# q weights in two requests ahead of x tiles 2 and 3, s one block behind y, and all reciprocals spread by way of DRAM

## Chip, cores and metric

The kernel runs on one core of one Trainium2 chip. The metric is the time of one execution on the device in microseconds (us). All times compared here are of undisturbed ("fast") runs.

## The reference

A layernorm of x feeds two branches, whose product is added to x. Branch A is attention with 32 heads of 16, over a window of 8 positions that are 2 apart. Branch B is a gated feed-forward net.

```python
x = A_x                                        # 1 x 2048 x 512, bf16
xn = _layernorm(x, axis=-1)
# branch A: idx = pos - 2 * [0..7], masked below 0
qkv = xn @ wqkv                                # 512 -> 3 * 512
logits = einsum("bhsd,bhswd->bhsw", q, k[idx]) * 16 ** -0.5
o = einsum("bhsw,bhswd->bhsd", softmax(logits), v[idx])
s = o @ wo                                     # 512 -> 512
# branch B
h = gelu(xn @ w_gate) * (xn @ w_up)            # 512 -> 1792
g = silu(h @ w_down)                           # 1792 -> 512
return x + s * g
```

## The kernel before

The 2048 positions are cut in two ways. A *tile of x* is 128 positions (there are 16: statistics, normalisation and transposition go by these). A *stage tile* is 512 positions, four tiles of x; there are four stage tiles, and for each of them the kernel does q/k/v, the attention sums, gate and up products ("glu"), and then, block by block of 128 positions, the down product y and the output product s. The order on each engine is the program's own: nothing is rescheduled. An engine takes its instructions in that order.

The loads, all issued in one queue by SyncE:

```python
for t in range(TPQ - 1):                 # x tiles 0, 1, 2: 128 KB each
    load_x(t)
load_w(wqkv_sb, A_wqkv, 0, D)            # q weights, 512 KB
load_x(TPQ - 1)                          # x tile 3
for i in range(1, 3):                    # k weights, v weights
    load_w(wqkv_sb, A_wqkv, i * D, (i + 1) * D)
load_x(TPQ, TPQ)                         # x tiles 4 to 7, then gate and up weights ...
```

The start-up. `warm_up` is idle matmuls, put there so that TensorE's clock comes up early (in the profile before, its matmuls of 128 columns start 0.106 us apart at 4.63 us and 0.056 us apart at 5.37). `first_moments` puts the statistics on VectorE and a square root on ScalarE. `transpose` is four transposes on TensorE into one PSUM tile, and a copy out of it, by ScalarE unless another is named; with `parts=2` the copy is made in two halves.

```python
first_moments(0); first_moments(1)
first_normalize(0)
transpose(0)
first_normalize(1)
warm_up(4, P)
transpose(1, parts=2)
warm_up(4, P)
first_moments(2); first_moments(3)
first_normalize(2); first_normalize(3)
# q of x tiles 0 and 1: 16 matmuls of 256 columns
...
transpose(HT, copy=nc.vector.tensor_copy)            # x tile 2
for fo in range(NC, 2 * NC):                         # k of x tiles 0 and 1
    qkv(0, fo, 0, HQ)
    if fo == NC:
        transpose(HT + 1, copy=nc.vector.tensor_copy)    # x tile 3
...
for fo in range(2 * NC):                             # q and k of x tiles 2 and 3
    qkv(0, fo, HQ, HQ)
```

The attention division: `denominators` sums the exponentials on TensorE and takes reciprocals on VectorE; these stand on 32 rows by head and have to be spread to all rows. For stage tiles 0 to 2 this goes through DRAM, for the last one by four matmuls:

```python
def spread_reciprocals(j):               # last stage tile
    sp = mm.tile([P, TQ], F32, name="sp_ps", tag="mm")
    for q in range(4):
        nc.tensor.matmul(sp[:, q * P : (q + 1) * P], lhsT=spread[:, q, :], rhs=st[j]["rs"][:], ...)
    rb = op.tile([P, TQ], F32, name="rb")
    nc.scalar.activation(out=rb[:], in_=sp[:], func=AF.Copy)

def spread_by_dma(j):                    # the others
    nc.sync.dma_start(out=rs_d[j][:, :], in_=st[j]["rs"][:])
    for i in range(WL):
        nc.sync.dma_start(out=rb[...], in_=rs_d[j]...)
```

The last stage, for each block of 128 positions:

```python
def down(j, tt):
    # y: 14 matmuls of 512 columns; sl = silu(y) on ScalarE
    # s: 4 matmuls of 512 columns from oT (the divided attention) and wo
    # m = s * sl, o_t = m + x on VectorE; store
```

The softmax here doesn't subtract the row's maximum and nothing guards it: scores larger than these inputs give would overflow.

## Time and profile before

| | before |
|---|---|
| time, median of 3 runs | 230.13 us (230.06 to 230.57) |
| span of the profiled execution | 228.7 us |
| TensorE busy, matmuls | 223.6 us, 98% |
| first q matmul | 7.00 us |
| first transpose of x tile 2 | 8.82 us |
| first k matmul | 9.06 us |
| first gate matmul | 18.20 us |

The last four rows are read from the timeline of TensorE. From the first gate matmul on TensorE has nearly no hole, so a delay at that station is a delay at the end. Two of the rows in the words of the timeline (start, length, engine, source line, operation, what it writes and reads, shape, count):

```profile
9.06 0.60 PE L247 MATMUL qkv_ps<-xnT,wqkv_sb 128*128 128x256 bf16 x4
...
18.20 1.03 PE L247 MATMUL g_ps<-xnT,wg_sb 128*128 128x512 bf16 x4
```

The DMA queue in the same start-up, from the view of busy time by stretch. The columns are the stretch and its length, then busy us and number of instructions of TensorE, its weight loads, VectorE, ScalarE and GpSimd, the granted clock, the busy share of the DMA engines, and GB/s moved.

```profile
3.50:4.50 1.00, 1.00 (x7) 0.67 (x5) 0.93 (x5) 0.29 (x1) 0.00 (x0) 1.00 0.78 115
4.50:7.00 2.50, 1.75 (x23) 1.27 (x21) 1.80 (x7) 1.66 (x5) 0.00 (x0) 1.00 1.03 359
```

The rate dips around 4 us, and is near 360 in the second stretch.

### The profile page before, as it was taken

The numbers are of one execution on the slowest core, as the hardware profiler recorded it, in microseconds if no ns is written. First come the engines' busy times: TensorE is split into PE (matmuls) and PEld (weight loads), VectorE is DVE, ScalarE is ACT, GpSimd is POOL, SyncE is SP. The second block draws the span as 40 slices with busy tenths as digits, with TensorE's granted clock in tenths as the row PEclk, the third lists the DMA queues.
The fourth block names the chain that finished last, engine by engine and source line by source line (L and its number), as shares of the span: only waits on it lengthen the run. The fifth ranks groups of instructions, "written<-read, shape, count | busy, mean of one in ns | idle before, by whom it ended". The sixth has DMA issues, their size and how long they took to land.

```text
span 228.7 us, 3538 instructions
## 1 busy us (share of the span) xinstructions
PE 223.6 (98%) x1324; PEld 106.3 (46%) x1324; DVE 147.6 (65%) x234; ACT 130.2 (57%) x214; POOL 23.0 (10%) x61
## 2 busy tenths in 40 slices
PE   8899999999999999999999999999999999999993
PEld 6764444444444444444444444444444444444453
DVE  4584996896995198865677169735549429945232
ACT  4679769764413866467621786747642396748211
POOL 1048973000000000110000000000000000000000
PEclk9999999999999999999999999999999999999999
DMA  6999589982378211110275711110147800000001
GB/s 163 359 373 371 140 170 199 242 204 75 109 172 197 55 24 29 26 29 0 92 175 135 170 25 28 26 34 0 45 120 165 203 26 3 0 0 4 23 23 46
DMA packets 30545, 24.46 MB, mean 107 GB/s; under 512 B 10176, under 2 KB 30528, under 8 KB 30528
## 3 DMA queue, kind: packets, MB, share of 16 engines
q1 hardware_dynamic: 30528, 24.24, 41.9%
q8 instruction: 10, 0.16, 0.3%
q14 instruction: 7, 0.06, 0.1%
HBM read 18.61 MB, written 4.31 MB: 100 GB/s over the span
## 4 chain that ended last, share of the span: by engine, by line
PE 94%; DMA 2%; ACT 1%; SPq 1%; DVE 0%; issue 0%; DVEq 0%
PE y_ps L416 21%; PE u_ps L247 21%; PE g_ps L247 21%; PE qkv_ps L247 17%; PE s_ps L426 6%; PE L_ps L304 3%; PE o_ps L375 3%; DMA wqkv_sb<-in_A_wqkv_dram 2%; PE q_ps L247 1%; ACT L400 1%; SPq L85 1%; PE den_ps L324 0%; ACT ge L400 0%; ACT vst L271 0%; PE tr L212 0%; ACT xnT L221 0%
## 5 line engine op out<-in xcount | busy, mean ns | idle before, releaser
L247 PE MATMUL g_ps<-xnT,wg_sb 128*128 128x512 bf16 x224 | 57.6, 379 | 0.0
L247 PE MATMUL u_ps<-xnT,wu_sb 128*128 128x512 bf16 x224 | 57.5, 379 | 0.0
L416 PE MATMUL y_ps<-wd_sb,h 128*128 128x512 bf16 (+1 forms) x238 | 51.2, 366 | 0.0
L404 DVE TENSOR_TENSOR h<-ge,u 128x512 bf16<-128x512 bf16 x56 | 23.8, 425 | 37.1 <-ACT u L402 36.4
L293 DVE TENSOR_TENSOR pk<-q_sb,k_sb 128x2048 bf16<-128x2048 bf16 x32 | 37.8, 1221 | 7.0 <-ACT k_sb L268 7.0
L402 ACT ACTIVATE u<-u_ps 128x512 bf16<-128x512 f32 x56 | 33.5, 599 | 14.7 <-PE u_ps L247 14.7
L400 ACT ACTIVATE ge<-g_ps 128x512 bf16<-128x512 f32 x56 | 33.5, 599 | 14.7 <-PE g_ps L247 14.4
L247 PE MATMUL qkv_ps<-xnT,wqkv_sb 128*128 128x512 bf16 (+1 forms) x208 | 40.9, 355 | 0.0
L361 DVE TENSOR_TENSOR pv<-E,v_arr 128x2048 bf16<-128x2048 bf16 x32 | 38.6, 1216 | 0.0
L416 PEld LDWEIGHTS <-h 128*128 128x128 bf16 x238 | 23.3, 98 | 25.3
L423 ACT ACTIVATE sl<-y_ps 128x512 bf16<-128x512 f32 (+1 forms) x17 | 9.7, 572 | 44.0 <-PE y_ps L416 44.0
L247 PEld LDWEIGHTS <-wu_sb 128*128 128x128 bf16 x224 | 21.9, 98 | 26.7 <-issue 0.3
L247 PEld LDWEIGHTS <-wg_sb 128*128 128x128 bf16 x224 | 21.2, 98 | 27.1 <-issue 3.0
L247 PEld LDWEIGHTS <-wqkv_sb 128*128 128x128 bf16 x224 | 21.6, 98 | 20.2 <-DMA wqkv_sb<-in_A_wqkv_dram 0.9
L434 DVE TENSOR_TENSOR m<-s_ps,sl 128x512 bf16<-128x512 f32 (+1 forms) x17 | 11.2, 658 | 24.2 <-PE s_ps L426 24.1
L426 PE MATMUL s_ps<-wo_sb,oT 128*128 128x512 bf16 (+1 forms) x68 | 16.6, 366 | 0.0
L197 POOL TENSOR_TENSOR rstd<-rstd,mhalf 128x1 f32<-128x1 f32 x12 | 7.7, 638 | 77.4 <-DVE rstd L194 75.2
L271 ACT ACTIVATE vst<-qkv_ps 128x512 bf16<-128x512 f32 x16 | 9.6, 597 | 6.4 <-PE qkv_ps L247 6.4
L268 ACT ACTIVATE k_sb<-qkv_ps 128x512 bf16<-128x512 f32 (+1 forms) x20 | 10.2, 514 | 3.5 <-PE qkv_ps L247 3.2
L265 ACT ACTIVATE q_sb<-qkv_ps 128x512 bf16<-128x512 f32 (+1 forms) x16 | 8.7, 544 | 3.6 <-PE qkv_ps L247 3.3
L426 PEld LDWEIGHTS <-oT 128*128 128x128 bf16 x68 | 6.6, 98 | 7.2
L159 POOL COPY spread<-ident 32x32 bf16<-32x32 bf16 x16 | 9.7, 646 | 0.2
(52 smaller groups left out, 115.8 us busy)
## 6 DMA issues: line engine op xcount, KB each, us to landing
v_arr<-vT SPq DMA_DIRECT2D x16, 520.0 KB, 5.1
vT<-vst SPq DMA_DIRECT2D x16, 128.0 KB, 2.1
out_dram<-o_t SPq DMA_DIRECT2D x15, 128.0 KB, 2.3
wg_sb<-in_B_w_gate_dram SPq DMA_DIRECT2D x2, 896.0 KB, 10.9
wu_sb<-in_B_w_up_dram SPq DMA_DIRECT2D x2, 896.0 KB, 12.7
wd_sb<-in_B_w_down_dram SPq DMA_DIRECT2D x1, 1792.0 KB, 13.7
wqkv_sb<-in_A_wqkv_dram SPq DMA_DIRECT2D x3, 512.0 KB, 5.6
x_sb<-in_A_x_dram SPq DMA_DIRECT2D x3, 512.0 KB, 11.4
```

Source lines behind the costliest of these rows:

```text
L159: nc.gpsimd.tensor_copy(out=spread[H * q : H * (q + 1), q, H * j : H * (j + 1)], in_=ident[H * q : H * (q + 1), H * q : H * (q + 1)],)
L247: nc.tensor.matmul(ps, lhsT=w[:, dk, lo : lo + P], rhs=xnT[j][:, dk, i0 : i0 + n], start=(dk == 0), stop=(dk == NC - 1),)
L268: nc.scalar.activation(out=k_sb[:, c, lo : lo + n], in_=ps, func=AF.Copy)
L293: nc.vector.tensor_tensor(out=pk[:], in0=st[j]["q"][:], in1=k_sb[:, :, off : off + TQ], op=ALU.mult)
L361: nc.vector.tensor_tensor(out=pv[:], in0=st[j]["E"][:, wh, :].unsqueeze(1).to_broadcast([P, 4, TQ]), in1=st[j]["va"][:, 4 * g : 4 * g + 4, ...
L400: nc.scalar.activation(out=ge[:], in_=g_ps[:], func=AF.Gelu_apprx_tanh)
L402: nc.scalar.activation(out=u[:], in_=u_ps[:], func=AF.Copy)
L404: nc.vector.tensor_tensor(out=h[:], in0=ge[:], in1=u[:], op=ALU.mult)
L416: nc.tensor.matmul(y[:], lhsT=st[j][fc][:, tt * P : (tt + 1) * P], rhs=wd_sb[:, fc, cols], start=(fc == 0), stop=(fc == NF - 1),)
L423: nc.scalar.activation(out=sl[:, cols], in_=y[:], func=AF.Silu)
L426: nc.tensor.matmul(s[:], lhsT=st[j]["oT"][:, g, tt * P : (tt + 1) * P], rhs=wo_sb[:, g, cols], start=(g == 0), stop=(g == NC - 1),)
L434: nc.vector.tensor_tensor(out=m[:], in0=s[:], in1=sl[:, cols], op=ALU.mult)
```

## The change

Its intent: the first matmul earlier (half of the q weights is asked for before x tile 2, and the last transposed tile is copied by two engines); fewer mode changes on TensorE (denominators and attention sums of stage tile 0 next to each other); four matmuls less (the last reciprocals go through DRAM as well); and s of a block one block later, so that it need not wait for its division. The core of the diff:

```diff
-    for t in range(TPQ - 1):
-        load_x(t)
-    load_w(wqkv_sb, A_wqkv, 0, D)
-    load_x(TPQ - 1)
+    load_x(0)
+    load_x(1)
+    load_w(wqkv_sb, A_wqkv, 0, D, 0, 2)      # rows 0 to 255 of the q weights
+    load_w(wqkv_sb, A_wqkv, 0, D, 2, 4)      # rows 256 to 511
+    load_x(2, 2)                             # x tiles 2 and 3 in one request
 ...
-            if copy is None:
+            if copy is None or k % 2:
                 nc.scalar.activation(out=dst[:, c], in_=src[:, c], func=AF.Copy)
             else:
                 copy(out=dst[:, c], in_=src[:, c])
 ...  # (the matmuls and the constants of spread_reciprocals go; every stage tile uses DRAM)
-    at(("qkv", 1, 3), denominators, 0)
-    at(("qkv", 1, 3), spread_by_dma, 0)
-    at(("qkv", 1, 10), av_sums, 0)
-    at(("qkv", 1, 10), divide, 0)
+    at(("qkv", 1, 8), denominators, 0)
+    at(("qkv", 1, 8), av_sums, 0)
+    at(("qkv", 1, 8), store_reciprocals, 0)
+    at(("qkv", 1, 10), spread_reciprocals, 0)
+    at(("down", 0, 0), divide, 0)
 ...
-    transpose(1, parts=2)
+    transpose(1, parts=2, copy=nc.vector.tensor_copy)
 ...
-    transpose(HT, copy=nc.vector.tensor_copy)
     for fo in range(NC, 2 * NC):
         qkv(0, fo, 0, HQ)
-        if fo == NC:
-            transpose(HT + 1, copy=nc.vector.tensor_copy)
+        if fo < NC + 2:
+            transpose(HT + fo - NC, copy=nc.vector.tensor_copy)
 ...  # down() is split: y and its silu in down(), s, product, sum and store in finish()
+        todo = []
         for tt in range(TPQ):
             run("down", j, tt)
-            down(j, tt)
+            ...
+                sl = down(j, tt, cols)
+                if todo:
+                    finish(*todo.pop())
+                ...
+                    todo.append((j, tt, cols, sl))
```

Cut from it: the new place of three pk products and some pv products on VectorE, and the last block, whose two halves keep the old order.

More of the change, by code (lines that the diff above doesn't have):

```diff
@@ L81 @@
     vT = dram.tile([D, SV], BF16, name="vT")
-    rs_d = [dram.tile([P, P], BF16, name=f"rs_d{j}") for j in range(NJ - 1)]
+    rs_d = [dram.tile([P, P], BF16, name=f"rs_d{j}") for j in range(NJ)]
     def load_x(t, n=1):
@@ L88, in load_x, with load_w @@
         )
-    def load_w(dst, src, lo, hi):
+    def load_w(dst, src, lo, hi, k0=0, k1=NC):
         nc.sync.dma_start(
-            out=dst[:, :, lo:hi], in_=src.rearrange("(k p) n -> p k n", p=P)[:, :, lo:hi]
-        )
-    for t in range(TPQ - 1):
-        load_x(t)
-    load_w(wqkv_sb, A_wqkv, 0, D)
-    load_x(TPQ - 1)
+            out=dst[:, k0:k1, lo:hi],
+            in_=src.rearrange("(k p) n -> p k n", p=P)[:, k0:k1, lo:hi],
+        )
+    load_x(0)
[3 more added lines that the diff above has]
+    load_x(2, 2)
     for i in range(1, 3):
@@ L140 @@
     hsum = const.tile([P, H], BF16, name="hsum")
-    spread = const.tile([P, 4, P], BF16, name="spread")
     dsum = const.tile([P, NC, H], BF16, name="dsum")
@@ L155, in sum_constants @@
             )
-        nc.gpsimd.memset(spread[:], 0.0)
-        for q in range(4):
-            for j in range(4):
-                nc.gpsimd.tensor_copy(
-                    out=spread[H * q : H * (q + 1), q, H * j : H * (j + 1)],
-                    in_=ident[H * q : H * (q + 1), H * q : H * (q + 1)],
-                )
     xnT = {}
@@ L334, in denominators, with store_reciprocals @@
         st[j]["rs"] = rs
+    def store_reciprocals(j):
+        nc.sync.dma_start(out=rs_d[j][:, :], in_=st[j]["rs"][:])
     def spread_reciprocals(j):
-        sp = mm.tile([P, TQ], F32, name="sp_ps", tag="mm")
-        for q in range(4):
-            nc.tensor.matmul(
-                sp[:, q * P : (q + 1) * P], lhsT=spread[:, q, :], rhs=st[j]["rs"][:],
-                start=True, stop=True,
-            )
-        rb = op.tile([P, TQ], F32, name="rb")
-        nc.scalar.activation(out=rb[:], in_=sp[:], func=AF.Copy)
-        st[j]["rb"] = rb
-    def spread_by_dma(j):
-        nc.sync.dma_start(out=rs_d[j][:, :], in_=st[j]["rs"][:])
-        rb = op.tile([P, TQ], BF16, name="rbd")
+        rb = op.tile([P, TQ], BF16, name="rb")
         for i in range(WL):
@@ L405, in glu @@
         st[j][fc] = h
-    def down(j, tt):
-        t = j * TPQ + tt
-        halves = [slice(0, D // 2), slice(D // 2, D)] if t == NT - 1 else [slice(0, D)]
-        n = D // len(halves)
-        sl = sm2.tile([P, D], BF16, name="sl")
-        o_t = sm4.tile([P, D], BF16, name="o_t")
-        for i, cols in enumerate(halves):
-            y = mm.tile([P, n], F32, name="y_ps", tag="mm")
-            for fc in range(NF):
-                nc.tensor.matmul(
-                    y[:],
-                    lhsT=st[j][fc][:, tt * P : (tt + 1) * P],
-                    rhs=wd_sb[:, fc, cols],
-                    start=(fc == 0),
-                    stop=(fc == NF - 1),
-                )
-            nc.scalar.activation(out=sl[:, cols], in_=y[:], func=AF.Silu)
-            s = mm.tile([P, n], F32, name="s_ps", tag="mm")
-            for g in range(NC):
-                nc.tensor.matmul(
-                    s[:],
-                    lhsT=st[j]["oT"][:, g, tt * P : (tt + 1) * P],
-                    rhs=wo_sb[:, g, cols],
-                    start=(g == 0),
-                    stop=(g == NC - 1),
-                )
-            m = sm2.tile([P, n], BF16, name="m")
-            nc.vector.tensor_tensor(out=m[:], in0=s[:], in1=sl[:, cols], op=ALU.mult)
-            nc.vector.tensor_tensor(out=o_t[:, cols], in0=m[:], in1=x_sb[:, t, cols], op=ALU.add)
-            nc.sync.dma_start(out=out2d[t * P : (t + 1) * P, cols], in_=o_t[:, cols])
@@ new lines, in down @@
+    def down(j, tt, cols):
+        n = cols.stop - cols.start
+        y = mm.tile([P, n], F32, name="y_ps", tag="mm")
+        for fc in range(NF):
+            nc.tensor.matmul(
+                y[:],
+                lhsT=st[j][fc][:, tt * P : (tt + 1) * P],
+                rhs=wd_sb[:, fc, cols],
+                start=(fc == 0),
+                stop=(fc == NF - 1),
+            )
+        sl = sm.tile([P, n], BF16, name="sl")
+        nc.scalar.activation(out=sl[:], in_=y[:], func=AF.Silu)
+        return sl
@@ new lines, in finish @@
+    def finish(j, tt, cols, sl):
+        t, n = j * TPQ + tt, cols.stop - cols.start
+        s = mm.tile([P, n], F32, name="s_ps", tag="mm")
+        for g in range(NC):
+            nc.tensor.matmul(
+                s[:],
+                lhsT=st[j]["oT"][:, g, tt * P : (tt + 1) * P],
+                rhs=wo_sb[:, g, cols],
+                start=(g == 0),
+                stop=(g == NC - 1),
+            )
+        m = sm2.tile([P, n], BF16, name="m")
+        nc.vector.tensor_tensor(out=m[:], in0=s[:], in1=sl[:], op=ALU.mult)
+        o_t = sm4.tile([P, n], BF16, name="o_t")
+        nc.vector.tensor_tensor(out=o_t[:], in0=m[:], in1=x_sb[:, t, cols], op=ALU.add)
+        nc.sync.dma_start(out=out2d[t * P : (t + 1) * P, cols], in_=o_t[:])
@@ L462 @@
     for i in range(8):
-        at(("glu", 0, 12 + i) if i < 2 else ("qkv", 1, (0, 1, 3, 4, 5, 6)[i - 2]),
+        at(("glu", 0, 11 + i) if i < 3 else ("qkv", 1, (0, 1, 2, 4, 5)[i - 3]),
            av_product, 0, i // 2, i % 2)
-    at(("qkv", 1, 3), denominators, 0)
-    at(("qkv", 1, 3), spread_by_dma, 0)
-    at(("qkv", 1, 10), av_sums, 0)
-    at(("qkv", 1, 10), divide, 0)
+    at(("qkv", 1, 8), denominators, 0)
[3 more added lines that the diff above has]
+    at(("down", 0, 0), divide, 0)
     for j in range(1, NJ):
         for w in range(W):
-            early = j > 1 and w < 3
-            at(("qkv", j, 9 + w) if early else ("down", j - 1, w // 3), qk_product, j, w)
+            at(("qkv", j, 9 + w) if w < 3 else ("down", j - 1, w // 3), qk_product, j, w)
         for i in range(TPQ):
@@ L480 @@
         at(("glu", j, 11), av_sums, j)
-        if j + 1 < NJ:
-            at(("glu", j, 11), spread_by_dma, j)
-            at(("qkv", j + 1, 6), divide, j)
-        else:
-            at(("glu", j, 12), spread_reciprocals, j)
-            at(("glu", j, 13), divide, j)
+        at(("glu", j, 11), store_reciprocals, j)
+        at(("glu", j, 11), spread_reciprocals, j)
+        at(("qkv", j + 1, 6) if j + 1 < NJ else ("down", j, 0), divide, j)
     HT = TPQ // 2
@@ L538 @@
                 qkv(j + 1, i)
+        todo = []
         for tt in range(TPQ):
             run("down", j, tt)
-            down(j, tt)
+            last = j * TPQ + tt == NT - 1
+            for cols in (slice(0, D // 2), slice(D // 2, D)) if last else (slice(0, D),):
+                sl = down(j, tt, cols)
+                if todo:
+                    finish(*todo.pop())
+                if last:
+                    finish(j, tt, cols, sl)
+                else:
+                    todo.append((j, tt, cols, sl))
+        if todo:
+            finish(*todo.pop())
 _INS = ['A_x', 'A_wqkv', 'A_wo', 'B_x', 'B_w_gate', 'B_w_up', 'B_w_down']
```

## The prediction

> **What bounds the kernel now.** I read the busy shares of the page first, then the chain of work that ended last, then the timeline of the first 19 us and of the last 30 us.
>
> ```profile
> PE 223.6 (98%) x1324; PEld 106.3 (46%) x1324; DVE 147.6 (65%) x234; ACT 130.2 (57%) x214; POOL 23.0 (10%) x61
> PEclk9999999999999999999999999999999999999999
> PE 94%; DMA 2%; ACT 1%; SPq 1%; DVE 0%; issue 0%; DVEq 0%
> ```
>
> TensorE is busy for 98% of the span at full clock and holds 94% of the chain; the other engines are far from full. A busy TensorE is not yet a full one, so I looked at the pitch of the matmuls in the chain:
>
> ```profile
> 2.19 4.76 DMA wqkv_sb<-in_A_wqkv_dram
> 6.95 0.05 issue
> 7.00 1.92 PE q_ps L247 x16
> 8.91 0.31 PE tr L212 x4
> ...
> 44.91 2.59 PE qkv_ps L247 x12
> 47.50 0.23 PE den_ps L324 x8
> 47.73 6.15 PE qkv_ps L247 x28
> 53.87 1.84 PE o_ps L375 x32
> 55.72 1.83 PE qkv_ps L247 x8
> 57.55 3.02 PE y_ps L416 x14
> 60.57 0.86 PE s_ps L426 x4
> ...
> 94.03 0.23 PE den_ps L324 x8
> 94.25 1.73 PE o_ps L375 x32
> 95.98 0.97 PE g_ps L247 x4
> ...
> 205.96 0.22 PE sp_ps L339 x4
> ```
>
> Four 512-wide matmuls take 0.86 us and fourteen take 3.02, so 0.216 us each, in every stage and also where y hands over to s. No row of y or s is stretched: moving s cannot win a wait, because there is none. From the first q matmul at 7.00 to the last s at 225.24 I find one hole, 0.2 us near 21.1 (a table load on ScalarE delays the release of a PSUM bank); the change does not touch it. What is left is 7 us of start-up, some mode changes and 3.5 us of tail.
>
> The start-up, from the timeline (start, length, what, idle before):
>
> ```profile
> 5.57 1.18 ACT L221 ACTIVATE xnT<-tr 128x512 bf16<-128x512 bf16 x3 [0.66 <-PE tr L212]
> 7.36 0.69 DVE L181 BATCH_NORM_STATS2 stats<-x_sb 128x6 f32<-128x512 bf16 x1 [0.95 <-DMA x_sb<-in_A_x_dram]
> 8.35 0.41 DVE L203 TENSOR_SCALAR xn<-x_sb,mv,rstd 128x512 bf16<-128x512 bf16 x1
> 8.95 1.21 ACT L265 ACTIVATE q_sb<-q_ps 128x256 bf16<-128x256 f32 x4 [0.35 <-PE q_ps L247]
> ```
>
> Copies of the first two transposed tiles end at 6.75 on ScalarE; the q weights land at 6.95; so the weights hold the first matmul by some 0.25 us only. Tile 3 of x lands just before 7.36, which is 4.7 us after its issue at 2.66. Tile 2's normalisation ends at 8.76, in time for its transpose at 8.82.
>
> **The Trainium skill.** "Perfetto Trace Analysis", Identifying the Most-Contended Engine, says that matmul busy share does not tell how near TensorE is to its limit; hence the pitch above. "TensorE: Matmul & The Clock Gate", Back-to-back issue gap, gives N/2.4 + 2.5 ns for an isolated gap, 216 ns at N = 512, but a lower sustained figure of about 131 ns; this trace shows 216 everywhere, so it agrees with the first only, and I take 0.216. "TensorEngine Tiling (Array Packing)", Key Properties, says that a change of tiling mode drains TensorE. The trace agrees: o takes 1.73 when it follows den (the same 128x32 mode) and 1.84 when it follows 128x128 work, and the group after it 0.97 for 0.86: 0.11 us per change. "DMA: Bandwidth & Descriptors", Queues, rings and completion order, says that each DMA engine takes its ring's descriptors in order. So a request's landing depends on the bytes ahead of it, and splitting one changes little for those behind.
>
> **Part 1: reciprocals of the last tile by DRAM.** Four sp matmuls go: 0.22 us off the path. The ScalarE copy of 0.59 us and 16 GpSimd copies (9.7 us) go too, all beside the path. In their place the last tile gets a store and four loads. In this kernel a store of reciprocals lands 1.5 us and a spread load 1.7 us after issue (medians). The reciprocal ends at 204.2, four issues at 0.45 us follow the store, so the spread lands near 204.2 + 1.5 + 1.4 + 2 = 209. The division (2.35 us) then ends by about 213, and s is wanted only after two y blocks, at about 209.4 + 6.0 = 215.4. Hidden. Gain 0.22.
>
> **Part 2: denominators and sums of tile 0 together.** From 44.91 to 57.55 is 12.64 us; the q/k/v stage of tile 1, without den and o, takes 10.36 (48 matmuls). So den and o cost 2.28 apart. Together, as at 94.03: 0.23 + 1.73 + 0.11 = 2.07. Gain 0.21. They now begin after 8 of the 12 groups, at about 51.8. The last of the eight pv products should end near 53.0 on VectorE (the last now ends at 53.9, with a 0.95 us reciprocal among them that moves behind), and the last step of o is due at about 53.55. Margin half a microsecond. The division waits for the spread, which I put at about 60.3, and ends near 62.7; s of the first block is due at 63.4. Close, but the first half of the division frees the first two matmuls of s.
>
> **Part 3: s one block behind y.** The same 16 groups, in another order. y and s have no waits now, so 0. Stores leave one block later except in the last tile, whose last y, s, multiply, add and store stay as they are: the tail is unchanged.
>
> **Part 4: start-up.** The first half of the q weights goes out third and not fourth. x tile 1's half copy on VectorE can run beside ScalarE: tile 0's copy 5.57 to 6.17; tile 1's transpose ends about 6.05, VectorE's half ends about 6.35, ScalarE's at about 6.55. The first eight q matmuls can start at about 6.42, if the first half has landed. Weights used to start moving behind three x tiles, now behind two: about 0.45 us earlier, and half of them is 256 KB, so I estimate 5.8 at worst. So the first matmul moves from 7.00 to 6.42, 0.58 us earlier.
>
> But this must last. Tiles 2 and 3 of x are now one request of 256 KB behind all 512 KB of q weights. The bytes up to its end are the same 1 MB as up to the end of tile 3 before, so I estimate its landing at about 7.25 instead of 7.34. Before, tile 2 had been measured long before; now two tiles are measured one after the other from 7.25: the second statistics begin 0.83 later, and by the old spacing (7.36 to 8.76, so 1.40 from its second statistics to the normalised tile 2) the normalised tile 2 is there at 7.25 + 0.83 + 1.40 = 9.48. TensorE wants it after 16 q matmuls and the first k group, at 6.42 + 1.92 + 0.43 = 8.77 (the k weights, about 8.7, take most of 0.4 of that difference already). So it stands still for some 0.7 us. It is not over then: ScalarE's queue has the two square roots ahead of the q copies, so those start at about 9.3 (8.95 before), and the first k copy ends at 9.3 + 1.21 + 0.39 = 10.9, which is what the fourth k group waits for (its PSUM bank). That group then ends at about 11.42. Before, the same place in TensorE's order was 9.88 + 1.30 = 11.18. So the earlier start is more than used up: +0.24 us. With a landing at 7.0 it would be about 0; TensorE alone, without any wait, would give -0.58.
>
> **Sum.** -0.22 (sp) - 0.21 (mode changes) + 0 (s) + 0.24 (start-up) = -0.2 us. The start-up is lopsided towards a gain, since landings of 6.7 to 7.4 are all credible and lie mostly below 7.34; with a mean of +0.1 the sum is -0.33. 230.13 - 0.33 = 229.8.
>
> **The rivals.** (a) The earlier start survives: x tiles land at 6.5 because weights start earlier into an idle queue, and TensorE hardly waits: -0.58 - 0.43 = -1.0, 229.1. For it: the DMA queue is slow in the first 5.7 us (163 GB/s against 359 in the next slice), so there is room. Against it: the queue is in order and the bytes ahead of tile 3 are unchanged. (b) The joined request lands later, at 7.6 or so, by a slow DMA engine among the 16: start-up +0.6, total +0.2, 230.3. For it: one request waits for its slowest engine. (c) A new wait at tile 0's sums or division: v lands late, VectorE is full there (10.77 us busy of 12.6 between 44.9 and 57.5), and a missed margin costs up to 1 us: 230.8. Against it: the margins of 0.5 and 0.7 us worked out above. (d) s behind y wins a wait: this would need stretched rows of s or y, and there are none.
>
> **Range and chances.** (a) and (b) span 229.1 to 230.3, and the three runs of before spread 0.5 us; (c) is at perhaps one in ten. I take 229.2 to 230.5. Two per cent is 4.6 us, and all of start-up and tail that could move is less than half of that; within 2% is almost sure.
>
> **What would show it.** Right: first q matmul near 6.4; a TensorE gap of 0.5 to 1 us before the first transpose of x tile 2, put down to its normalisation, and a shorter one at the fourth k group, put down to ScalarE; the second halves of q and k starting within 0.4 us of 11.2; den and o of tile 0 adjacent, o at 1.73; no sp rows; y and s rows still at 0.216 us a matmul, no gap before s of the last tile. Wrong: no gap behind the first k group (then a), gaps inside o or before s of tile 0 (then c), or a first matmul still at 7.0, which would mean that the weights' landing does not follow the order of issue.

## The result, and the profile after

| | before | after |
|---|---|---|
| time, median (6 runs each, same chip) | 230.12 us (229.93 to 230.57) | 230.82 us (230.72 to 231.15) |
| ratio after / before | | 1.0029, 95% interval 1.0016 to 1.0043 |
| profiled span | 228.7 us | 228.9 us |
| first q matmul | 7.00 | 7.13 |
| first k matmul | 9.06 | 9.28 |
| first transpose of x tile 2 | 8.82 | 9.86 |
| first gate matmul | 18.20 | 18.81 |
| from there to the end | 210.5 | 210.1 |

A ratio is the mean time of one kernel's fast runs over that of the other's of the same rounds, so it is not quite the ratio of the medians quoted. By it the change costs 0.67 us; predicted was a gain of 0.33. That is "within 2%", but on the other side of zero and above the range. The profiled spans differ by 0.2 us only. That pair flatters the change: on the chip of the first experiments the spans of the kernel before lay between 228.2 and 229.0, with a median of 228.5 (on another chip they reached 229.6), so one profile of 228.7 is not its typical value.

The table divides the loss already: up to the first gate matmul 0.61 us are lost, from there to the end 0.4 us are won. The page after, with its busy shares and the chain of work that ended last:

```profile
PE 223.1 (97%) x1300; PEld 106.9 (47%) x1320; DVE 147.8 (65%) x235; ACT 129.5 (57%) x212; POOL 12.8 (6%) x44
...
PE 92%; DMA 3%; ACT 2%; SPq 1%; issue 1%; DVE 0%; ACTq 0%; DVEq 0%
```

TensorE works 0.5 us less (223.1 for 223.6) while the span is not shorter, and its share of the chain falls from 94 to 92%: the difference is TensorE standing still. The same chain in order of time (start, length, what) shows where:

```profile
3.21 6.03 DMA wqkv_sb<-in_A_wqkv_dram
9.24 0.05 issue
9.28 0.61 PE qkv_ps L241 x4
...
52.48 0.23 PE den_ps L318 x8
52.70 1.73 PE o_ps L360 x32
...
57.99 6.04 PE y_ps L397 x28
64.03 0.86 PE s_ps L413 x4
```

The first piece is new. Before, the chain began with the landing of the *q* weights at 6.95; now it begins with the landing of the *k* weights at 9.24. Further down, the steps that were to gain are as intended: den and o are adjacent with o at 1.73, there is no row of sp, two y blocks run without a break and s follows at once.

The start-up in the timeline after:

```profile
6.69 0.29 DVE L217 COPY xnT<-tr 128x256 bf16<-128x256 bf16 x1 [1.04 <-PE tr L206]
7.02 0.38 ACT L215 ACTIVATE xnT<-tr 128x256 bf16<-128x256 bf16 x1 [0.58 <-DVE xnT L217]
7.13 1.91 PE L241 MATMUL q_ps<-xnT,wqkv_sb 128*128 128x256 bf16 x16
7.60 0.69 DVE L175 BATCH_NORM_STATS2 stats<-x_sb 128x6 f32<-128x512 bf16 x1 [0.62 <-DMA x_sb<-in_A_x_dram]
9.28 0.61 PE L241 MATMUL qkv_ps<-xnT,wqkv_sb 128*128 128x256 bf16 x4 [0.25 <-DMA wqkv_sb<-in_A_wqkv_dram]
9.38 0.41 DVE L197 TENSOR_SCALAR xn<-x_sb,mv,rstd 128x512 bf16<-128x512 bf16 x1
9.86 0.40 PE L206 MATMUL tr<-ident,xn 128*128 128x128 bf16 x4
```

Read it from top to bottom. The two half copies do not run side by side: ScalarE's idle time before its half is ended by VectorE's half, and it begins at 7.02, just after that ended at 6.98. The first q matmul is at 7.13, 0.15 us after VectorE's half ended; ScalarE's half is still running then, as the first eight q matmuls need the first half only. Tiles 2 and 3 land just before 7.60, the k weights at 9.24, and the transpose of tile 2 waits for a normalisation that ends at 9.79.

And the DMA queue after, in the same two stretches as before:

```profile
3.50:4.50 1.00, 1.00 (x7) 0.67 (x5) 0.93 (x4) 0.29 (x1) 0.00 (x0) 1.00 1.05 367
4.50:7.00 2.50, 2.50 (x22) 2.05 (x20) 1.37 (x6) 0.89 (x2) 0.00 (x0) 1.00 0.81 248
```

Against before, the dip of the first stretch is gone (367 for 115; a shorter one has moved ahead of it, 92 and 159 GB/s in the slices from 3.0 to 3.4 us), and a second one has come: 248 GB/s for 359. The second stretch alone overstates the loss, for the changed kernel had moved more before it: from 0 to 7.0 us the mean is 192 GB/s for 202.

### The profile page after: what moved, and what is told of

It is laid out like the page before. It is cut to its first block, busy times and chain, and to the rows that moved or that the text cites. A ratio compares the mean times of both kernels' runs of the same rounds, so it can differ in the third digit from the quotient of the medians.

```text
span 228.9 us, 3496 instructions
## 1 busy us (share of the span) xinstructions
PE 223.1 (97%) x1300; PEld 106.9 (47%) x1320; DVE 147.8 (65%) x235; ACT 129.5 (57%) x212; POOL 12.8 (6%) x44
## 4 chain that ended last, share of the span: by engine, by line
PE 92%; DMA 3%; ACT 2%; SPq 1%; issue 1%; DVE 0%; ACTq 0%; DVEq 0%
PE u_ps L241 21%; PE y_ps L397 21%; PE g_ps L241 19%; PE qkv_ps L241 17%; PE s_ps L413 6%; PE L_ps L298 3%; PE o_ps L360 3%; DMA wqkv_sb<-in_A_wqkv_dram 3%; ACT u L387 1%; ACT L385 1%; SPq L85 1%; SPq L91 0%; PE den_ps L318 0%; ACT ge L385 0%; ACT vst L265 0%
## 5 line engine op out<-in xcount | busy, mean ns | idle before, releaser
L241 PE MATMUL g_ps<-xnT,wg_sb 128*128 128x512 bf16 x213 | 56.3, 379 | 0.4
L397 PE MATMUL y_ps<-wd_sb,h 128*128 128x512 bf16 (+1 forms) x236 | 50.2, 366 | 0.1
L413 PE MATMUL s_ps<-wo_sb,oT 128*128 128x512 bf16 (+1 forms) x66 | 15.8, 366 | 0.2
L372 DVE TENSOR_TENSOR oT<-o_ps,rb 128x1024 bf16<-128x1024 f32 x8 | 9.4, 1216 | 2.8 <-DMA rb<-rs_d 2.8
```

The source lines that it names most:

```text
L241: nc.tensor.matmul(ps, lhsT=w[:, dk, lo : lo + P], rhs=xnT[j][:, dk, i0 : i0 + n], start=(dk == 0), stop=(dk == NC - 1),)
L397: nc.tensor.matmul(y[:], lhsT=st[j][fc][:, tt * P : (tt + 1) * P], rhs=wd_sb[:, fc, cols], start=(fc == 0), stop=(fc == NF - 1),)
L413: nc.tensor.matmul(s[:], lhsT=st[j]["oT"][:, g, tt * P : (tt + 1) * P], rhs=wo_sb[:, g, cols], start=(g == 0), stop=(g == NC - 1),)
```

## The experiments

Fifteen runs were made (two of them repeat the kernels before and after): the first four below on one chip, the next four on another, the ninth to the twelfth on a third, the rest on a fourth. All outputs are right. Each was timed against the kernel before on its own chip in five rounds, so "ratio" is always to the kernel before, with the 95% interval in brackets. A comparison of two experiments by their ratios is good to some 0.2 to 0.3%. 0.1% is 0.23 us. The rest alone (e4), to which many are compared, was timed once, on the first chip. The profile of each is a single execution, and not always a typical one: those of the start-up alone (e3) and of the requests (e5) are the fastest of their six runs, that of the changed kernel's repeat (e2) the second fastest. The spans of e3 go from 228.8 us, the profiled one, to 230.2.

### The two kernels again

No edit; this shows how far single profiles vary.

> The kernel before, unchanged, for its spans in several runs and a second profile. In the first profile of before the first q matmul started at 7.00 and the span was 228.7 at 230.45 us, at the upper end of its times (229.93 to 230.57). Theory start-up (all of the loss lies ahead of the first gate matmul): a typical run of before has a shorter start-up than the one profiled, spans near 228.3, ratio 1.000. Rival chance (the two profiles differ by when the TensorE clock came up, 4.77 us in before and 6.79 in after, and that is luck): this profile may show a clock that comes up near 6.8 too, and the times fall into two groups some 0.4 to 0.5 us apart that go with it.

> The changed kernel, unchanged, for a second profile. Theory start-up: ratio 1.003, first gate matmul again near 18.8 with tile 2 and 3 of x landing near 7.5 and the k weights near 9.2. Rival chance: if the clock comes up early here, the first q matmul starts near 6.5 and the landings alone remain.

Measured: the kernel before against itself 1.0002 [0.9989, 1.0015]; the changed kernel 1.0021 [1.0005, 1.0038]. So the loss is real and small, 0.2 to 0.3%. The profiles showed two things that one look had hidden. First, in the first profile of before x tile 3 landed at 7.34; in this one it landed at 6.64. Neither is an outlier: in the seven profiles with these requests it landed at 6.64 to 7.34, in three of them after 7.1. In two of the later experiments, e6 and e12, the statistics of tile 3 begin as soon as it has landed, and late:

```profile
7.19 0.69 DVE L173 BATCH_NORM_STATS2 stats<-x_sb 128x6 f32<-128x512 bf16 x1 [0.79 <-DMA x_sb<-in_A_x_dram]
```

```profile
7.29 0.69 DVE L181 BATCH_NORM_STATS2 stats<-x_sb 128x6 f32<-128x512 bf16 x1 [0.82 <-DMA x_sb<-in_A_x_dram]
```

Second, TensorE's full clock came up at 6.79 in the first profile of after (its four transposes at 5.19 took 0.61 instead of 0.40), and at 5.05 in this one. Now the first q matmul of the changed kernel is at 6.65, earlier than 6.78 of before; still its first gate matmul is later, at 18.21 against 17.98. So the late clock is not the whole cause. It came up late again in two of the later profiles, at 6.59 in the start-up alone and at 6.74 in a kernel with uncut q weights (e13), so it looks like chance; how often it happens in the executions that were not profiled is not known.

### The start-up alone, and the rest alone

The first has all of the start-up's edits (loads, half copy, order of transposes) in the kernel before. The second has the changed kernel with the start-up of before:

```diff
 # rest only, against the changed kernel
-    load_x(0); load_x(1)
-    load_w(wqkv_sb, A_wqkv, 0, D, 0, 2); load_w(wqkv_sb, A_wqkv, 0, D, 2, 4)
-    load_x(2, 2)
+    for t in range(TPQ - 1):
+        load_x(t)
+    load_w(wqkv_sb, A_wqkv, 0, D)
+    load_x(TPQ - 1)
 ...  # and the half copy and the transposes as before
```

> Before with only the start-up part of the change (requests, half copy on VectorE, order of transposes). Theory start-up: it costs all of the loss and what the other parts win, so +0.7 + 0.43 = +1.1 us, ratio 1.0048. Rival rest (the other parts do not win what the chain shows, and the start-up costs what the profiles differ by, 0.6): +0.6, ratio 1.0026.

> After with the start-up of before (s behind y, reciprocals by DRAM, denominators with the sums). Theory start-up: -0.22 for the sp matmuls and -0.21 for two mode changes, so -0.43 us, ratio 0.998, 229.7 us, the fastest of the four. Rival rest: 0 to +0.1, ratio 1.000.

Measured: start-up alone 1.0052 [1.0034, 1.0070], a loss of 1.2 us; the rest alone 0.9979 [0.9966, 0.9992], a gain of 0.48 us, median 229.73 (229.62 to 229.80). The two add up to +0.7, which is what the whole change shows. The rest alone is the fastest kernel and beats both originals. Its start-up, from the timeline of TensorE:

```profile
6.56 1.91 PE L239 MATMUL q_ps<-xnT,wqkv_sb 128*128 128x256 bf16 x16 [0.24 <-ACT xnT L213]
8.30 0.39 PE L204 MATMUL tr<-ident,xn 128*128 128x128 bf16 x4
8.53 0.60 PE L239 MATMUL qkv_ps<-xnT,wqkv_sb 128*128 128x256 bf16 x4
17.67 1.03 PE L239 MATMUL g_ps<-xnT,wg_sb 128*128 128x512 bf16 x4
```

The old start-up, on a good day, has the first q matmul at 6.56, without any of the edits that were to bring it there; what it waits for is ScalarE's copy and not the q weights. That is the copy of the first half of tile 1, which begins 0.03 us after tile 1's transposes end (6.09) and is over at 6.50:

```profile
6.12 0.38 ACT L213 ACTIVATE xnT<-tr 128x256 bf16<-128x256 bf16 x1
```

### The parts of the start-up, one at a time

Each of these is the rest alone plus one part of the start-up.

```diff
 # e5: the requests                       # e6: order of the transposes
-    for t in range(TPQ - 1): load_x(t)   -    transpose(HT, ...)        # ahead of the k groups
-    load_w(wqkv_sb, A_wqkv, 0, D)        -        if fo == NC:
-    load_x(TPQ - 1)                      -            transpose(HT + 1, ...)
+    load_x(0); load_x(1)                 +        if fo < NC + 2:
+    load_w(..., 0, D, 0, 2)              +            transpose(HT + fo - NC, ...)
+    load_w(..., 0, D, 2, 4)
+    load_x(2, 2)                         # e8: e5, but
                                          -    load_x(2, 2)
 # e7: half copy on VectorE               +    load_x(2)
-    transpose(1, parts=2)                +    load_x(3)
+    transpose(1, parts=2, copy=nc.vector.tensor_copy)
```

> The kernel with the start-up of before (0.9979 of before, spans 227.7 to 227.9) plus only the changed requests: q weights in two halves ahead of one request for x tiles 2 and 3. Theory landing (what costs is that tile 2 arrives with tile 3 behind the weights, and is measured late): the joined request lands near 6.95, the normalised tile 2 comes 2.23 us behind it, the transpose of tile 2 slips from 8.3 to about 9.2 and the first gate matmul from 17.7 to about 18.6; +0.9 us over the start-up of before, so +0.4 over before, ratio 1.002. Rival order (the loss comes from the transposes standing behind the first k group, whose weights land late): the requests alone cost nothing or win, ratio 0.997 to 0.998.

> Start-up of before plus only the changed order of the transposes (first k group ahead of the transpose of tile 2). Theory landing: tile 2 is ready early here, so only the wait for the k weights (landed at 8.2 to 8.8 so far, wanted at 8.5) can cost: 0 to +0.3 us, ratio 0.998 to 0.9995. Rival order: +0.9, ratio 1.002.

> Start-up of before plus only the half copy on VectorE. The first q matmul started at 6.56 behind the ScalarE half; with VectorE beside it the copies are ready some 0.2 us earlier, but the q weights land at 6.3 and later. Both theories: -0.2 to 0 us, ratio 0.997 to 0.998. If VectorE's half stands in the way of something, slower.

> As the requests alone, but x tiles 2 and 3 are two requests again, both still behind the q weights. Theory landing: tile 2 lands about 0.35 us before tile 3 and is measured then; the transpose of tile 2 comes at about 8.85 instead of 9.2, so 0.3 to 0.4 us better than with the joined request, ratio 1.0005. If joining makes no difference, the same ratio as with the joined request.

Measured:

| | ratio | median us | expected ratio |
|---|---|---|---|
| requests (e5) | 1.0051 [1.0034, 1.0068] | 231.32 | 1.002 |
| transposes (e6) | 0.9996 [0.9984, 1.0008] | 230.09 | 0.998 to 0.9995 |
| half copy (e7) | 1.0006 [0.9994, 1.0018] | 230.34 | 0.997 to 0.998 |
| requests, x tiles separate (e8) | 1.0033 [1.0020, 1.0046] | 231.07 | 1.0005 |

Against 0.9979 of the rest alone, the requests cost 0.72% (1.7 us), the half copy 0.27% (0.6 us) and the transposes 0.17% (0.4 us, within what two ratios can differ by). Together with the rest they cost 0.4 to 0.5%, so they don't add up. A likely reason, argued and not shown, is that they delay the same chain, so that a wait for one covers the other. Asking for the x tiles separately (e8) makes one more issue, of 0.47 us, ahead of the k weights, which land at 9.93 there.

The half copy was expected to gain and costs. VectorE's lines of the rest alone and of the half copy, from the timeline, show why:

```profile
5.55 0.69 DVE L173 BATCH_NORM_STATS2 stats<-x_sb 128x6 f32<-128x512 bf16 x1
```

```profile
6.19 0.29 DVE L215 COPY xnT<-tr 128x256 bf16<-128x256 bf16 x1 [0.49 <-PE tr L204]
6.40 0.68 DVE L173 BATCH_NORM_STATS2 stats<-x_sb 128x6 f32<-128x512 bf16 x1
```

The copy stands in VectorE's queue ahead of the statistics of x tile 2 and waits there 0.49 us for the transpose. Tile 2 has landed meanwhile, but its statistics begin at 6.40 instead of 5.55. Its transpose then starts at 8.64 for 8.30 and the first gate matmul at 18.02 for 17.67. The first q matmul gains nothing, 6.63 for 6.56. It needs the first half only, and that copy begins 0.03 us after the transposes on either engine (6.19 after 6.15 on VectorE, 6.12 after 6.09 on ScalarE, whose copy of tile 0 is all but over by then); from its start to the first q matmul it is 0.44 us in both. So there was nothing for VectorE to take off ScalarE. The second halves do not run side by side with the first either: ScalarE's half follows VectorE's (6.51 after 6.48). But it is over at 6.90, before the ninth q matmul, the first to need it, starts at 7.50. The Trainium skill, "PSUM — Partial Sum Buffer", PSUM bank collisions raise a hardware error, says that two engines may not access the same bank and quadrant at once, and that the compiler's back end adds a dependency between them, ScalarE and VectorE included. Both halves are in one PSUM tile, and the trace agrees: in all seven profiles with the half copy ScalarE's half starts after VectorE's has ended. (Both halves also write the one tile xnT; which of the two made the dependency is not shown.)

### x tile 2 first

My theory after these was that the late landing of tile 2, which is now joined to tile 3 behind all q weights, does the harm. This undoes that alone in the changed kernel:

```diff
     load_x(0)
     load_x(1)
+    load_x(2)
     load_w(wqkv_sb, A_wqkv, 0, D, 0, 2)
     load_w(wqkv_sb, A_wqkv, 0, D, 2, 4)
-    load_x(2, 2)
+    load_x(3)
```

> The changed kernel with one thing undone: x tile 2 is requested ahead of the two halves of the q weights, tile 3 alone behind them. Theory landing: tile 2 is measured by about 6.9 again and only tile 3 depends on the end of the queue, where the kernel before had slack; most of the loss goes: first gate matmul near 18.0, 0.4 to 0.8 us less than the changed kernel, ratio to before 0.998 to 1.000, and the scatter of spans shrinks from 1 us to about 0.5. Rival split (two weight requests instead of one delay the k weights behind them, and that is the cost): ratio stays at 1.002 to 1.003.

Measured: 1.0051 [1.0030, 1.0072], no better than the whole change. The theory fell. The first k matmul is now as late as 9.65, and the timeline says what for:

```profile
9.65 0.61 PE L242 MATMUL qkv_ps<-xnT,wqkv_sb 128*128 128x256 bf16 x4 [1.22 <-DMA wqkv_sb<-in_A_wqkv_dram]
```

Two things are learnt. Tile 2's early landing is of little use, because on VectorE its normalisation stands behind tile 3's statistics. And what comes late is everything behind the cut weights, the k weights too.

### The cut alone, and the halves with tile 2 between

Both are the rest alone with the q weights in two requests, nothing else joined or moved behind them except as shown:

```diff
 # e10                                    # e11
     load_x(0); load_x(1); load_x(2)      load_x(0); load_x(1)
-    load_w(wqkv_sb, A_wqkv, 0, D)        load_w(wqkv_sb, A_wqkv, 0, D, 0, 2)
+    load_w(wqkv_sb, A_wqkv, 0, D, 0, 2)  load_x(2)
+    load_w(wqkv_sb, A_wqkv, 0, D, 2, 4)  load_w(wqkv_sb, A_wqkv, 0, D, 2, 4)
     load_x(3)                            load_x(3)
```

> Start-up of before (with the other parts of the change), only the q weights cut into two requests, both behind x tile 2. Theory landing: no more than 0.2 us either way against the uncut request, ratio 0.996 to 0.999. Rival split: k weights land some 0.5 us later, ratio 1.000 or more.

> As the run with the cut weights, but the first half of the weights goes ahead of x tile 2, the second behind it. Theory landing: tile 2 lands near 5.7 to 6.0, is measured in time, and the first q matmul still waits for the copies at 6.56, so as the cut alone, ratio 0.996 to 0.999. If any weights ahead of tile 2 cost, ratio 1.001 or more.

Measured: the cut alone 1.0032 [1.0007, 1.0057], with tile 2 between 1.0027 [1.0005, 1.0049]. I had expected 0.996 to 0.999 for the cut: the same bytes in the same order should land at the same time. It costs about 0.5%, 1.2 us, against the rest alone, and differs from it by one thing, that 512 KB are asked for in two requests of 256 KB. That brings one more issue with it, so all that lies behind is asked for some 0.5 us later (the k weights at 3.68 for 3.21); the two effects were not separated. Its timeline of TensorE, to be held against that of the rest alone above:

```profile
6.62 1.91 PE L242 MATMUL q_ps<-xnT,wqkv_sb 128*128 128x256 bf16 x16 [0.24 <-ACT xnT L216]
9.03 0.40 PE L207 MATMUL tr<-ident,xn 128*128 128x128 bf16 x4 [0.49 <-DVE xn L198]
9.92 0.61 PE L242 MATMUL qkv_ps<-xnT,wqkv_sb 128*128 128x256 bf16 x4 [0.50 <-DMA wqkv_sb<-in_A_wqkv_dram]
19.07 1.03 PE L242 MATMUL g_ps<-xnT,wg_sb 128*128 128x512 bf16 x4
```

The first q matmul is where it was (6.62 for 6.56). The first k matmul waits for its weights and comes 1.4 us later, and so does the first gate matmul. The DMA queue from 4.5 to 7 us, first of the rest alone, then of the cut alone:

```profile
4.50:7.00 2.50, 1.97 (x27) 1.60 (x25) 2.14 (x8) 1.66 (x5) 0.00 (x0) 1.00 1.07 358
```

```profile
4.50:7.00 2.50, 2.26 (x26) 1.73 (x25) 1.91 (x7) 1.62 (x5) 0.00 (x0) 1.00 0.83 215
```

The later issue alone does not explain the low rate: in the cut alone the q, k and v weights and four x tiles, 2 MB, had all been asked for by 4.7 us, when 0.8 MB had moved (167 GB/s from 0 to 5.0 us).

### s behind y alone

The kernel before with `down` split into `down` and `finish` as in the change, nothing else.

> Before with only s one block behind y. Nothing waits at y or s in before, so 0: ratio 1.000, within the interval. Rival: the move wins part of the 0.48 us that the other parts together won (0.9979), ratio 0.9985 or less.

Measured: 1.0007 [0.9987, 1.0028]. Nothing that shows, as predicted; the interval leaves room for 0.3 us of gain.

### The place alone, k weights in halves, the half copy later

The first is the rest alone with the requests in the new order but the q weights whole. The second is the changed kernel with the k weights cut as well. The third is the half copy of e7, with the statistics of x tile 2 ahead of it in VectorE's queue.

```diff
 # e13, against the rest alone            # e14, against the changed kernel
-    for t in range(TPQ - 1): load_x(t)   -    for i in range(1, 3):
+    load_x(0); load_x(1)                 -        load_w(wqkv_sb, A_wqkv, i * D, (i + 1) * D)
     load_w(wqkv_sb, A_wqkv, 0, D)        +    load_w(wqkv_sb, A_wqkv, D, 2 * D, 0, 2)
-    load_x(TPQ - 1)                      +    load_w(wqkv_sb, A_wqkv, D, 2 * D, 2, 4)
+    load_x(2, 2)                         +    load_w(wqkv_sb, A_wqkv, 2 * D, 3 * D)
 # e15, against e7
-    transpose(1, parts=2, copy=nc.vector.tensor_copy)
-    warm_up(4, P)
     first_moments(2)
+    transpose(1, parts=2, copy=nc.vector.tensor_copy)
+    warm_up(4, P)
```

> Start-up of before (with the other parts), x tiles 2 and 3 as one request behind the q weights, which stay ONE request. Theory dry queue (cutting the q weights lets them through early, then the queue runs dry until the k weights, still a 512 KB request issued at 3.21 us, come at full rate; in the cut kernels 1158 to 1396 KB had moved by 7.0 us against 1317 to 1405 in the uncut): no second dip, 1.35 MB or more by 7.0, k weights at 8.2 to 8.8, but tile 2 measured late, so about +0.6 us over the start-up of before: ratio 1.000 to 1.001. Rival place (a late tile 2 alone explains the requests' loss): as the cut requests, 1.004 to 1.005.

> The changed kernel with the k weights cut into two requests as well. Theory dry queue in its simple form (a smaller weights request reaches full rate sooner after its issue): the dip at 5 to 7 us gets shallower, k weights land no later although one more request stands in the queue, ratio 1.000 to 1.002. Rival (each further request costs 0.47 us of issue for all that follow, and that is what starves the queue): k weights later by about 0.4, ratio 1.004 to 1.006.

> Start-up of before (with the other parts) with the half copy on VectorE, which cost 0.27% against that start-up when it stood ahead of the statistics of tile 2 in VectorE's queue; here those statistics go first. If the cost was that VectorE stood waiting for the transposed tile 1 until 6.2 with tile 2's statistics behind it: ratio 0.998, as without the half copy. If the half copy costs in another way: 1.0005 or so again.

Measured: place alone 1.0010 [0.9998, 1.0022]; k weights in halves 1.0023 [1.0011, 1.0035]; half copy later 1.0008 [0.9994, 1.0021].

The place alone against the requests of e5 (1.0051), where only the cut differs, gives the price of the cut a second time: 0.41%, 0.9 us (here too with one more issue ahead of all that lies behind, the k weights at 3.21 for 2.74). The new place and the joined x tiles cost the other 0.31% (0.7 us) over the rest alone. The queue of the place alone keeps the old rate after the first dip; that of e14 does not:

```profile
4.50:7.00 2.50, 2.47 (x22) 2.10 (x21) 1.43 (x6) 1.21 (x4) 0.00 (x0) 1.00 1.08 361
```

```profile
4.50:7.00 2.50, 1.93 (x25) 1.51 (x24) 1.44 (x7) 1.27 (x3) 0.00 (x0) 1.00 0.84 284
```

If every further request of 256 KB made the queue slower, e14 should have been slower than the changed kernel; it isn't (1.0023 against 1.0021 and 1.0029). Its k weights are whole at 8.94, between the 8.43 and 9.24 of the changed kernel's two profiles, with one more issue ahead of their second half, so one more issue need not cost 0.5 us. Its rate of 284 lies between the changed kernel's 248 and 337. It settles nothing about the mechanism.

The half copy later was expected at 0.998, as its statistics are no longer held up. It stays at 1.0008: now the copy waits for the statistics, VectorE's half begins at 6.50 for 6.19, and the first q matmul is at 6.91 for 6.56. On VectorE one of the two is late in either order, and there was no wait of ScalarE's to win, so the copy by two engines loses either way here.

## Why the prediction was wrong

**Parts 1 to 3 (reciprocals by DRAM, den beside o, s behind y) were right.** Predicted -0.22 - 0.21 + 0 = -0.43; measured -0.48 (-0.8 to -0.2) for the three together and nothing that shows for the third alone. Parts 1 and 2 were not run apart; that both came about is seen in the chain after, where den and o stand together with o at 1.73 and no row of sp is left. The margins held as worked out: the division of stage tile 0 ran from 60.8 to 63.1, where I had 60.3 to 62.7, and s started at 63.87 in the timeline. Rival (c), a new wait there, and rival (d) did not happen.

**Part 4, the start-up, is the step that failed.** The prediction worked out +0.24, reckoned with +0.1, and so let the gain of parts 1 to 3 decide the sign. Measured was +1.2 alone, and +1.0 to +1.15 on top of the rest (1.0021 and 1.0029 against 0.9979). The step that failed is that a request cut in two changes little for those behind it; the runs show that they come later, at a price of 0.9 to 1.2 us. By its terms:

- *"splitting one changes little for those behind"*. This sentence, drawn from the order of descriptors in a ring, is the costliest error: 0.9 us (e5 against e13, give or take 0.5) to 1.2 us (e10 against e4, give or take 0.6) when nothing but the cut, with its one more issue, differs. Order of service fixes the bytes ahead of a request, not the time at which the last of them is there. In the profiles with the q weights whole the queue moved 342 to 370 GB/s from 4.5 to 7 us; with them cut 215 to 337. The highest of the cut ones, 337, is the second look at the changed kernel, so the dip varies from execution to execution. From 0 to 7.0 us the two kinds lie closer, 193 to 215 and 169 to 204. That its loss comes by way of late k weights and late x tile 3 is seen in the waits. What is late of them is in the table below. Why, is not settled.
- *"x tile 1's half copy on VectorE can run beside ScalarE"*. It doesn't: ScalarE's half starts after VectorE's in every profile. But the first q matmul does not wait for that; it follows VectorE's half by 0.15 us (6.50 to 6.65, 6.98 to 7.13), and 6.42 was not reached because tile 1's transposes ended at 6.18 and 6.65, not at 6.05, and because 0.07 was reckoned for these 0.15. The 6.75 that the prediction took for the copies' end was the end of the second half; the first half was over at 6.47 in that very profile, so a copy by two engines had at most 0.1 us to win. What it costs, 0.27% alone, is its place in VectorE's queue, ahead of tile 2's statistics.
- *"I estimate its landing at about 7.25 instead of 7.34"*. The baseline was a single sample, and the latest of seven: with the same requests tile 3 landed at 7.34, 7.27, 7.16, 6.88, 6.68, 6.67 and 6.64. In the four profiles with the requests of the change (after, e2, e3, e5) the joined tiles landed at 6.93, 6.94, 6.98 and 7.57. So 7.25 was well inside what came; on the mean the joined tiles are 0.15 later than tile 3 was, where 0.1 earlier was reckoned. The remark that the start-up "is lopsided towards a gain" rested on this sample and was the wrong way round.
- *The wait for the k weights* was named ("the k weights, about 8.7") and thought to be absorbed. They landed at 9.24 in the first profile of the changed kernel and at 8.43 in the second, and in the changed order TensorE waits for them before it comes to tile 2's transpose. The predicted second stand-still at the fourth k group did not appear.

The arithmetic from a landing onwards was good: it put the end of the four k groups at the landing plus 4.17, so at 11.74 and 11.15 for the landings of 7.57 and 6.98. The second q halves then started at 11.64 and 11.04. In the first of these the k weights were late as well, so that agreement is partly luck; and the last piece of the 4.17 was the wait for ScalarE, which did not appear in either.

Rival (b), a joined request that lands later "by a slow DMA engine among the 16", was right in direction and in kind. The kept traces have 16 increments for each request, of which the views show only the last; I take them for one from each of the 16 DMA engines, which the trace does not name. At what time the 8th, the 15th and the 16th came, in us:

| | x tile 3 (joined with tile 2 in the changed kernel): 8th, 15th, 16th | k weights: 8th, 15th, 16th |
|---|---|---|
| before | 6.50, 6.69, 7.34 | 8.01, 8.18, 8.80 |
| rest alone (e4) | 6.38, 6.57, 6.68 | 7.95, 8.06, 8.16 |
| after | 6.05, 6.51, 7.57 | 7.93, 9.00, 9.24 |
| after again (e2) | 6.15, 6.97, 6.98 | 7.81, 8.42, 8.43 |
| cut alone (e10) | 6.19, 7.30, 7.54 | 8.78, 9.65, 9.88 |

In all nine profiles with cut q weights half of tile 3 was there earlier than in the seven with the old requests (6.05 to 6.30 for 6.33 to 6.68), but the last share came at 6.93 to 8.14 for 6.64 to 7.34, in five of the nine later than in any of the seven. So what is late is mostly not the queue as a whole (it is for the k weights of the cut alone, 8.78 for 7.95) but some of a request's 16 shares, and the request has landed when the last of them has. Rival (b) put the cost at +0.6, half of what was measured, and did not tie it to the cut.

**Not settled:** why some shares come late behind two requests of 256 KB and less so behind one of 512 KB, and how much of it is the one more issue. All kernels dip once between 3 and 4.5 us; the uncut ones recover for good, and the cut ones dip again (the second profile of the changed kernel hardly, with 337). Cutting the next weights too (e14) made it neither worse nor plainly better. Nor does any profile show the whole loss: in the three profiles of the changed start-up (after, e2, e3) the first gate matmul is at 18.81, 18.21 and 18.24, in the three of the kernel before with its old start-up (before, e1, e12) at 18.20, 17.98 and 18.13, which is 0.3 us on the mean and near the +0.24 worked out. The times say 0.7 to 1.2 us; what the slower executions did was not profiled.

## What to carry to other kernels

When a start-up is bound by landings, judge a reordering of requests by when the last share of each request is there and by what lies *behind* the piece that was brought forward, not only by the bytes ahead of it. Before taking a landing from a profile as the baseline, see it in other executions: here the same request's landings spread over 0.7 us, three times what was at stake. And a piece of work that is moved to a "free" engine stands in that engine's queue: ask what it holds up there, and whether the engine that it relieves was late at all.

## What the Trainium skill lacked or had wrong

- "DMA: Bandwidth & Descriptors", Queues, rings and completion order: it gives the order of service, and Rules for kernel authors calls transfers under 64 KB mostly overhead and asks for 1 MiB or more for the highest bandwidth. Nothing says that cutting a 512 KB request into two of 256 KB can cost the requests behind it 0.9 to 1.2 us at the start of a kernel, with the queue at 215 to 337 GB/s where it moved 342 to 370 uncut.
- "TensorE: Matmul & The Clock Gate", Part 1: it puts the transition around 4 us, give or take half a microsecond (and adds that it varies by run). In 17 profiles with the same idle matmuls from 0.84 us on the record of the granted clock begins to show full speed between 3.62 and 6.79 us, that is 2.8 to 6.0 us into them, a wider spread than the page's (in the last case matmuls of 128 columns still start 0.107 us apart at 6.66, where 0.056 is full speed). In the three profiles with 6.59 or later the first q matmul is at about 7.1, in the others at 6.5 to 7.0.
- The same page, Back-to-back issue gap: the sustained 131 ns for 512 columns was seen nowhere in these kernels; long streams ran at 216 ns throughout, which is the page's formula for an isolated matmul, and also what Part 1 of the page has for back-to-back matmuls.
- "TensorEngine Tiling (Array Packing)", Key Properties: it gives no figure for the drain at a change of mode. Here rows next to such a change are 0.11 us longer (1.84 for 1.73, 0.97 for 0.86), and putting two such pieces together was part of a measured gain of 0.48 us.
